# Landmark attention and a gated FFN on one core: landmark exchange in 256-byte pieces, Bm normalised from PSUM, R and a copy of Bm from one matmul, reciprocals kept in PSUM, and a new order of the stages

## The chip, the core and the metric

The kernel runs on one NeuronCore of a Trainium2 chip. Five engines work side by side, each through its own instructions in order: PE (TensorE, matmuls), DVE (VectorE), ACT (ScalarE), POOL (GpSimd) and SP (SyncE, which here only issues DMA transfers). They meet through semaphores. PE reads SBUF and writes PSUM; DVE and ACT read and write both; POOL reads and writes SBUF alone. The metric is device time in microseconds, the median of the runs shown; one more execution was profiled.

## What is computed

Eight batches of eight heads of attention with 32 landmarks, then a multiplicative FFN over all 4608 tokens:

```python
def _attn_ref(q, k, v):                       # (8, 8, 576, 64) each
    m = 32
    scale = 1.0 / np.sqrt(D)
    q_lm = q.reshape(B, H, m, S // m, D).mean(axis=3)
    k_lm = k.reshape(B, H, m, S // m, D).mean(axis=3)
    ...
    A = sm(q, k_lm)                           # softmax of scaled products
    Bm = sm(q_lm, k_lm)
    C = sm(q_lm, k)
    Z = Bm.transpose(0, 1, 3, 2) / (norm1(Bm) * norminf(Bm) + 1e-06)
    for _ in range(6):
        Z = 2 * Z - Z @ Bm @ Z
    return A @ Z @ C @ v

def _moe_ref(x, w1, w2, w3, w_out):           # x: 4608 x 512
    a = x @ w1
    b = x @ w2
    h = a * b @ w3
    return h @ w_out
```

## The kernel before

The program works batch by batch (number after the dot), and its order is written out by hand: ORDER is a list of 569 words, each of which emits the instructions of one stage on all the engines that the stage uses. Every engine then runs its instructions in the order in which the words emitted them, and there is no scheduler. The words, with the lines of the code before:

- LK, LQ (L105): load k or q of a batch as f16 through POOL's queue. LV (L124, L128): load v through SP's queue, four transfers. Two buffers each, so the load of batch b+2 waits until the readers of batch b are done.
- TK0, TK1, TQ0, TQ1 (L140): DVE transposes half of k or q in 32x32 blocks into qkT.
- SK, SQ (L189 to L195): POOL adds up the 18 tokens of each landmark, six instructions, into the tile lm (f16).
- E (L200): exchange. Each group of 32 partitions needs the landmark half that its neighbour group made. Four transfers from lm to lm on SP's queue move them, in pieces of 64 bytes (the 32 values of one head pair). They wait for POOL's last addition.
- B (L215 to L229): PE multiplies the landmarks of q and k into PSUM (small), ACT takes exp into SBUF (ebm), DVE sums (rbs), inverts, multiplies to bm and transposes to bt.
- C0, C1 (L242, L248, L250): landmarks of q against k, exp with a sum, transpose. A0, A1 (L289, L294): q against landmarks of k, exp.
- N (L256 to L265): column sums of bm by a matmul, their maximum inverted (nrn), and bm times nrn into the right half of sz. R (L274 to L280): bt times bt by 16 small matmuls; DVE scales the result into the left half of sz and adds 2I into tz.
- I0 to I5 (L363 to L373): the six steps of the iteration for Z, a chain PE, then DVE (tz) and ACT (sz), then PE.
- V0 to V2 (L310 to L322): exp(C) times v. D (L328): row sums of A into psD (small). Y0 to Y2 (L336): DVE inverts a third of them each, into rr in SBUF. X (L340, L342): DVE casts rr to f16 (rhi) and makes the mixed tile rmix. M0, M1 (L348, L351): PE spreads rmix, DVE multiplies A.
- Z (L380 to L386), G0 to G3 (L400 to L406): landmark values times w1 and w2. U0a to U7b (L413 to L419): both FFN factors by PE, ACT copies one out (a_sb), DVE multiplies (ab). W0.n, W1.n (L435, L444): the last product for 128 tokens, evicted by ACT and stored by two transfers on SP's queue.
- F: one piece of the fold of w3 with w_out into a single weight (L457 to L480), 64 pieces, which fill PE early on.

PSUM holds three tiles `big` of two banks, one `small` and one `acc`. So each new `small` (of B, N, R, D, Z) waits until the last one has been read.

The early words of ORDER, up to the second exchange (L32 to L35 of the code before; P and L3 load pieces of w3):

```
... TK0.0 F TK1.0 L3.3 F F F TQ0.0 P.4 L3.5 SK.0 ... TQ1.0 ...
... LV.0 ... TK0.1 F F SQ.0 F E.0 F TK1.1 SK.1 F F F F B.0 C0.0 C1.0 F F F N.0 A0.0 A1.0
TQ0.1 LK.2 LQ.2 R.0 ... I5.0 M0.0 LK.3 LQ.3 Z.0 M1.0 SQ.1 F G0.0 G1.0 E.1 ...
```

Of the kernel before, what the change touches and what calls it, by code (L numbers as in the profile page):

```python
# [31 lines left out]
F F F F F F F F F F F F F TK0.0 F TK1.0 L3.3 F F F TQ0.0 P.4 L3.5 SK.0 F F F F F TQ1.0 F F F F F  # L32
F F LV.0 F F F F TK0.1 F F SQ.0 F E.0 F TK1.1 SK.1 F F F F B.0 C0.0 C1.0 F F F N.0 A0.0 A1.0
TQ0.1 LK.2 LQ.2 R.0 L3.6 F F F V0.0 TQ1.1 I0.0 F I1.0 F F L3.7 I2.0 V1.0 D.0 Y0.0 Y1.0 Y2.0 F F
I3.0 F I4.0 V2.0 F F X.0 I5.0 M0.0 LK.3 LQ.3 Z.0 M1.0 SQ.1 F G0.0 G1.0 E.1 F F F TK0.2 TK1.2  # L35
SK.2 B.1 A0.1 C0.1 C1.1 F N.1 G2.0 G3.0 A1.1 F F TQ0.2 F F U0a.0 R.1 U0b.0 U1a.0 U1b.0 TQ1.2
LV.1 U2a.0 U2b.0 D.1 V0.1 U3a.0 I0.1 TK0.3 TK1.3 I1.1 U3b.0 V1.1 I2.1 U4a.0 Y0.1 SQ.2 Y1.1 Y2.1
E.2 I3.1 LK.4 LQ.4 X.1 U4b.0 I4.1 V2.1 M0.1 I5.1 U5a.0 TQ0.3 U5b.0 U6a.0 M1.1 Z.1 U6b.0 U7a.0
U7b.0 LV.2 G0.1 G1.1 B.2 G2.1 G3.1 W0.0 N.2 C0.2 C1.2 W1.0 SK.3 U0a.1 U0b.1 W0.1 TQ1.3 U1a.1
U1b.1 U2a.1 V0.2 R.2 A0.2 A1.2 SQ.3 LV.3 TK0.4 TK1.4 E.3 W1.1 I0.2 U2b.1 D.2 I1.2 Y0.2 Y1.2 Y2.2  # L40
V1.2 U3a.1 I2.2 W0.2 TQ0.4 U3b.1 U4a.1 TQ1.4 V2.2 I3.2 X.2 W1.2 U4b.1 I4.2 M0.2 W0.3 I5.2 B.3
SK.4 A0.3 U5a.1 U5b.1 Z.2 U6a.1 U6b.1 G0.2 G1.2 W1.3 M1.2 LK.5 LQ.5 U7a.1 U7b.1 G2.2 G3.2 W0.4
U0a.2 N.3 U0b.2 C0.3 C1.3 W1.4 A1.3 R.3 U1a.2 U1b.2 V0.3 I0.3 W0.5 U2a.2 TK0.5 U2b.2 V1.3 U3a.2
D.3 SQ.4 TQ0.5 Y0.3 E.4 I1.3 Y1.3 Y2.3 W1.5 U3b.2 U4a.2 TQ1.5 V2.3 LV.5 I2.3 W0.6 U4b.2 I3.3
U5a.2 W1.6 LV.4 LK.6 LQ.6 X.3 I4.3 U5b.2 U6a.2 I5.3 W0.7 Z.3 M0.3 M1.3 W1.7 U6b.2 TK1.5 SK.5
SQ.5 U7a.2 U7b.2 G0.3 G1.3 W0.8 LK.7 LQ.7 B.4 A0.4 G2.3 G3.3 U0a.3 W1.8 N.4 C0.4 C1.4 E.5 A1.4
R.4 W0.9 U0b.3 U1a.3 W1.9 U1b.3 I0.4 TK0.6 V0.4 V1.4 U2a.3 U2b.3 TK1.6 W0.10 U3a.3 I1.4 D.4 Y0.4
Y1.4 Y2.4 V2.4 U3b.3 U4a.3 W1.10 I2.4 U4b.3 U5a.3 U5b.3 I3.4 W0.11 X.4 U6a.3 I4.4 U6b.3 SK.6
LV.6 A0.5 I5.4 W1.11 M0.4 M1.4 Z.4 U7a.3 U7b.3 G0.4 G1.4 B.5 W0.12 G2.4 G3.4 U0a.4 W1.12 N.5
C0.5 A1.5 R.5 C1.5 W0.13 U0b.4 W1.13 I0.5 TQ0.6 V0.5 V1.5 W0.14 TQ1.6 SQ.6 U1a.4 E.6 TK0.7 TK1.7  # L50
U1b.4 W1.14 I1.5 V2.5 U2a.4 D.5 Y0.5 Y1.5 I2.5 U2b.4 U3a.4 TQ0.7 W0.15 I3.5 Y2.5 U3b.4 U4a.4 X.5
W1.15 SK.7 I4.5 U4b.4 U5a.4 M0.5 W0.16 TQ1.7 I5.5 U5b.4 U6a.4 M1.5 Z.5 U6b.4 SQ.7 U7a.4 U7b.4
G0.5 G1.5 W1.16 E.7 B.6 A0.6 G2.5 G3.5 W0.17 W1.17 N.6 C0.6 C1.6 A1.6 R.6 W0.18 U0a.5 U0b.5
U1a.5 U1b.5 W1.18 I0.6 D.6 Y0.6 Y1.6 Y2.6 V0.6 U2a.5 W0.19 U2b.5 U3a.5 W1.19 I1.6 U3b.5 V1.6
I2.6 W0.20 X.6 I3.6 M0.6 W1.20 I4.6 V2.6 U4a.5 I5.6 U4b.5 U5a.5 M1.6 Z.6 U5b.5 U6a.5 B.7 G0.6
# [10 lines left out]
def kernel(  # L66
# [83 lines left out]
    def constants():  # L150
# [29 lines left out]
        return mask4, eye, eye2, onesq, selc, lomask  # L180


    def landmarks(st, t):
        if "lm" not in st:
            st["lm"] = pat.tile([128, 2, 4, 2, 16, 2], FP16, name="lm", bufs=3)
# [8 lines left out]
        for xh in range(2):  # L194
            add(out=st["lm"][:, t, :, xh], in0=o[:, :, :, 0, :], in1=o[:, :, :, 1, :], op=ALU.add)  # L195

    def exchange(st):
        for to in range(4):
            p, r = slice(32 * to, 32 * to + 32), slice(32 * (to ^ 1), 32 * (to ^ 1) + 32)
            nc.sync.dma_start(  # L200
                out=st["lm"][p, :, :, 1 - to % 2].rearrange("p t c l e -> p (t c) (l e)"),
                in_=st["lm"][r, :, :, 1 - to % 2].rearrange("p t c l e -> p (t c) (l e)"))

    def lmk(st, sl, t, pr, e):
        return st["lm"][sl, t, pr].rearrange("p x l e -> p (x l) e")[:, :, e]

    def scores_b(st):
        psB = small()
        for qd in range(2):
            for e in range(2):  # L210
                for o in range(4):
# [7 lines left out]
        ebm = pz.tile([128, 2, 32], FP32, name="ebm")  # L219
        nc.scalar.activation(out=ebm, in_=psB[:, 0:64].rearrange("p (a m) -> p a m", m=32),  # L220
                             func=AXF.Exp, scale=SCALE / (GRP * GRP))
        rbs = pz.tile([128, 2], FP32, name="rbs")
        nc.vector.reduce_sum(out=rbs, in_=ebm, axis=AX.X)
# [4 lines left out]
        bt = st["bt"] = pz.tile([128, 2, 32], FP32, name="bt")  # L228
        nc.vector.transpose(out=bt, in_=bm)  # L229
# [23 lines left out]
    def norms(st):  # L253
# [10 lines left out]
        sz_ = st["sz"] = pz.tile([128, 2, 64], FP32, name="sz_")  # L264
        nc.vector.tensor_tensor(out=sz_[:, :, 32:64], in0=bm,  # L265
                                in1=nrn.unsqueeze(2).to_broadcast([128, 2, 32]), op=ALU.mult)

    def squares(st):
        psR = small()
        bt, sz_ = st["bt"], st["sz"]  # L270
        for qd in range(2):
            for h in range(4):
                sl = slice(32 * h, 32 * h + 32)
                nc.tensor.matmul(psR[sl, 32 * qd:32 * qd + 32], bt[sl, qd, :], bt[sl, qd, :],  # L274
                                 start=True, stop=True, tile_position=(32 * h, 32 * h))
        nc.vector.tensor_tensor(out=sz_[:, :, 0:32],
                                in0=psR[:, 0:64].rearrange("p (a m) -> p a m", m=32),
                                in1=st["nrn"].unsqueeze(2).to_broadcast([128, 2, 32]), op=ALU.mult)
        tz_ = st["tz"] = pz.tile([128, 2, 32], FP32, name="tz_")
        nc.vector.tensor_tensor(out=tz_, in0=sz_[:, :, 0:32], in1=eye2, op=ALU.add)  # L280
# [43 lines left out]
    def denominators(st):  # L324
# [7 lines left out]
        st["rr"] = pat.tile([128, QS], FP32, name="rr", bufs=1)  # L332

    def inverted(st, i):
        sl = slice(QS // 3 * i, QS // 3 * (i + 1))
        nc.vector.reciprocal(out=st["rr"][:, sl], in_=st["psD"][:, sl])  # L336

    def mixed(st):
        rhi = pat.tile([128, QS], FP16, name="rhi", bufs=1)
        nc.vector.tensor_copy(out=rhi, in_=st["rr"])  # L340
        st["rmix"] = pat.tile([128, QS], FP16, name="rmix")
        nc.vector.scalar_tensor_tensor(out=st["rmix"], in0=rhi, scalar=lomask[:, 0:1], in1=st["rr"],  # L342
# [155 lines left out]
    sts = [dict() for _ in range(B)]  # L498
# [52 lines left out]
    mask4, eye, eye2, onesq, selc, lomask = constants()  # L551
# [92 lines left out]
```

## Time and profile before

| | us |
|---|---|
| median of 3 runs | 283.25 (282.9 to 284.06) |
| the profiled execution | 283.65 |
| its span, first to last instruction | 281.9 |
| busy: PE | 261.5 (93%) |
| busy: DVE | 183.2 (65%) |
| busy: ACT | 132.2 (47%) |
| busy: POOL | 104.3 (37%) |

Busy time is the union of an engine's instructions; waiting on semaphores and issuing transfers are not in it. The page lists for each group of instructions the count, the busy time and the mean duration of one; the view of waits lists who waited for whom; the view by windows gives each engine's busy time in a stretch, with the granted TensorE clock (1.00 is full speed) and the busy share of the 16 DMA engines. That share can read above 1, since packets overlap. The view of one line or one tile gives shortest, median and longest duration, and for transfers the time from issue to landing.

### The profile page before, as it was taken

The numbers are of one execution on the slowest core, as the hardware profiler recorded it, in microseconds if no ns is written. First come the engines' busy times: TensorE is split into PE (matmuls) and PEld (weight loads), VectorE is DVE, ScalarE is ACT, GpSimd is POOL, SyncE is SP. The second block draws the span as 40 slices with busy tenths as digits, with TensorE's granted clock in tenths as the row PEclk, the third lists the DMA queues.
The fourth block names the chain that finished last, engine by engine and source line by source line (L and its number), as shares of the span: only waits on it lengthen the run. The fifth ranks groups of instructions, "written<-read, shape, count | busy, mean of one in ns | idle before, by whom it ended". The sixth has DMA issues, their size and how long they took to land.

```text
span 281.9 us, 10481 instructions
## 1 busy us (share of the span) xinstructions
PE 261.5 (93%) x4572; PEld 148.9 (53%) x4572; DVE 183.2 (65%) x397; ACT 132.2 (47%) x285; POOL 104.3 (37%) x125
## 2 busy tenths in 40 slices
PE   7999977999889499989999999999999999999992
PEld 3554533554456165546655655665565565645640
DVE  6764223558988477987769866889775685465510
ACT  3642222425543354556358444744673655436531
POOL 0719545451569119970009960089500000000000
PEclk9999997999999799999999999999999999999998
DMA  7999998886008925699494198114232723133144
GB/s 252 301 244 278 254 241 204 138 144 172 2 6 118 226 63 157 117 174 209 110 273 112 13 216 240 40 42 84 44 67 57 185 62 74 44 77 77 37 114 113
DMA packets 31246, 37.91 MB, mean 134 GB/s; under 512 B 10976, under 2 KB 19168, under 8 KB 31200
## 3 DMA queue, kind: packets, MB, share of 16 engines
q1 hardware_dynamic: 20864, 24.26, 33.3%
q0 software_dynamic: 9536, 11.54, 24.9%
q10 hardware_dynamic: 800, 1.44, 1.4%
q8 instruction: 36, 0.59, 0.9%
q14 instruction: 10, 0.08, 0.1%
HBM read 38.80 MB, written 9.44 MB: 171 GB/s over the span
## 4 chain that ended last, share of the span: by engine, by line
PE 61%; DMA 16%; POOL 9%; DVE 7%; SPq 2%; issue 1%; ACT 1%; ACTq 0%; POOLq 0%; DVEq 0%
PE acc L435 18%; PE big L413 17%; DMA lm<-lm 10%; PE big L400 6%; PE acc L477 5%; POOL tr L189 4%; PE big L310 3%; PE big L363 3%; DMA qkn<-in_k_dram 3%; DMA wof<-in_moe_w_out_dram 2%; DVE qkT L140 2%; POOL tr L190 2%; SPq L200 2%; PE big L242 2%; PE big L348 1%
## 5 line engine op out<-in xcount | busy, mean ns | idle before, releaser
L413 PE MATMUL big<-ahat,gt 128*128 128x288 f16 x512 | 74.7, 287 | 0.4 <-ACT a_sb L417 0.4
L435 PE MATMUL acc<-w,ab 128*128 128x512 f16 x264 | 67.8, 383 | 0.1
L419 DVE TENSOR_TENSOR ab<-a_sb,big 128x576 f16<-128x576 f16 x64 | 48.0, 750 | 23.0 <-ACT a_sb L417 12.3
L189 POOL TENSOR_TENSOR tr<-qkT 128x1024 f32<-128x1024 f16 x16 | 34.0, 2127 | 74.4 <-DVE qkT L140 74.1
L417 ACT CAST a_sb<-big 128x576 f16<-128x576 f32 x64 | 40.9, 640 | 39.3 <-PE big L413 38.7
L413 PEld LDWEIGHTS <-gt 128*128 128x128 f16 x512 | 47.2, 98 | 21.2 <-issue 3.1
L477 PE MATMUL acc<-wsp,w3t 128*128 128x512 f16 x168 | 41.3, 387 | 0.7 <-ACT w L480 0.7
L435 PEld LDWEIGHTS <-ab 128*128 128x128 f16 x288 | 25.7, 98 | 27.9 <-issue 5.8
L477 PEld LDWEIGHTS <-w3t 128*128 128x128 f16 x192 | 18.4, 99 | 21.7 <-issue 4.3
L444 ACT ACTIVATE o_sb<-acc 128x512 f32<-128x512 f32 x33 | 19.7, 598 | 15.0 <-PE acc L435 14.2
L140 DVE STREAM_TRANSPOSE qkT<-qkn 128x576 uint32<-128x576 uint32 x32 | 24.0, 763 | 1.6 <-DMA qkn<-in_k_dram 1.6
L406 DVE TENSOR_SCALAR gt<-big 128x1024 f16<-128x1024 f32 x16 | 19.4, 1218 | 5.2 <-PE big L400 4.9
L470 DVE SCALAR_TENSOR_TENSOR w3t<-big,w3t 128x512 f16<-128x512 f32 x16 | 11.0, 690 | 17.2 <-ACT w3t L469 17.0
L190 POOL TENSOR_TENSOR tr<-tr 128x512 f32<-128x512 f32 x16 | 20.3, 1269 | 1.3
L404 ACT ACTIVATE gt<-big 128x1024 f16<-128x1024 f32 x16 | 16.4, 1024 | 8.6 <-PE big L400 8.6
L400 PE MATMUL big<-wup,zt 64*32 64x512 f16 x512 | 17.8, 394 | 0.8 <-DVE ab L419 0.8
L310 PE MATMUL big<-vt,ent 64*32 64x64 f32 x1152 | 16.6, 224 | 0.0
L469 ACT ACTIVATE w3t<-big 128x512 f16<-128x512 f32 x16 | 9.5, 594 | 13.0 <-PE big L464 12.9
L310 PEld LDWEIGHTS big<-vt,ent 64*32 64x32 f32 x1152 | 13.2, 105 | 3.6 <-issue 1.6
L248 ACT ACTIVATE en<-big 128x288 f32<-128x288 f32 x32 | 12.7, 412 | 2.6 <-PE big L242 2.6
L250 DVE STREAM_TRANSPOSE ent<-en 128x576 f32<-128x576 f32 x16 | 12.2, 772 | 2.5 <-ACT en L248 2.5
L195 POOL TENSOR_TENSOR lm<-tr 128x128 f16<-128x128 f32 x32 | 12.1, 400 | 1.3
(277 smaller groups left out, 291.1 us busy)
## 6 DMA issues: line engine op xcount, KB each, us to landing
vt<-in_v_dram SPq DMA_DIRECT2D x32, 288.0 KB, 5.1
out_dram<-o_sb SPq DMA_DIRECT2D x71, 128.0 KB, 2.4
qkn<-in_k_dram POOLq DMA_DIRECT2D x8, 576.0 KB, 6.5
qkn<-in_q_dram POOLq DMA_DIRECT2D x8, 576.0 KB, 8.6
w3f<-in_moe_w_dram SPq DMA_DIRECT2D x6, 512.0 KB, 7.2
wup<-in_moe_w_dram POOLq DMA_DIRECT2D x4, 512.0 KB, 26.8
wof<-in_moe_w_out_dram ACTq DMA_DIRECT2D x4, 256.0 KB, 5.7
wof<-in_moe_w_out_dram SPq DMA_DIRECT2D x4, 256.0 KB, 4.1
```

Of the source, the lines that this page charges most:

```text
L140: nc.vector.transpose(out=st["qkT"][:, t, prs].rearrange("p c r q e -> p (c r q e)").bitcast(U32), in_=st["qkn"][:, t, prs, :].rearrange(" ...
L189: add(out=tr, in0=x[:, :, 0:4, :], in1=x[:, :, 4:8, :], op=ALU.add)
L190: add(out=tr[:, :, 0:2, :], in0=tr[:, :, 0:2, :], in1=tr[:, :, 2:4, :], op=ALU.add)
L310: nc.tensor.matmul(psV[32 * o:32 * o + 32, qd, 0:64], ent[sl, pr, r, :], vt[sl, pr, 64 * r:64 * r + 64], start=(r == 0), stop=(r == RT - 1 ...
L400: nc.tensor.matmul(psG[32 * h:32 * h + 32, qd, :], zt[rs, i, h, :], wup[rs, h, w, fs], start=(i == 0), stop=(i == 1), tile_position=(64 * ...
L406: nc.vector.tensor_scalar(out=g[:, :, w, fs], in0=psG, scalar1=1.0 / ZS, scalar2=None, op0=ALU.mult)
L413: nc.tensor.matmul(p[:, c, 0:HS], st["g"][:, qd, w, 128 * j:128 * j + 128], st["ahat", qd][:, c, :], start=(qd == 0), stop=(qd == 1))
L417: nc.scalar.copy(out=st["a_sb"], in_=p[:, :, 0:HS])
L419: nc.vector.tensor_tensor(out=st["ab"][:, j, st["t0"]:st["t0"] + S].rearrange("p (c s) -> p c s", c=2), in0=st["a_sb"], in1=p[:, :, 0:HS], ...
L435: nc.tensor.matmul(pso[:, :], ab[:, j, t0:t0 + 128], w34[:, j, :], start=(j == 0), stop=(j == 7))
L444: nc.scalar.activation(out=o_sb[:, c], in_=pso[:, c], func=AXF.Copy, scale=1.0 / (X64 * X64))
L477: nc.tensor.matmul(psW[j][:, :], turned[j, c // 4][:, a, c % 4, :], wsp[:, b, c, :], start=(c == 0 and a + b == 0), stop=(c == 7 and a == 1))
```

## The change

Five things are changed.

1. The tile lm is laid out anew, [tensor][half][landmark][head pair][parity] in place of [tensor][head pair][half][landmark][parity]. The half that a partition group sends is then 256 contiguous bytes for each of q and k. The exchange is still four transfers of 16 KB in all 64 KB, each from 32 partitions, with 64 pieces in place of 256. POOL's last additions write, and the matmuls of A, B and C read, the tile with a step of 8 elements (16 bytes) where it was 2 (4 bytes).
2. B: the exponentials go into PSUM, beside the scores in the same bank, by two ACT instructions with an accumulated sum in place of one without. The DVE sum goes. bm is made from PSUM. bt is the left half of one of two constant tiles whose right half is the identity.
3. N and R: the DVE product bm times nrn in N goes. The 16 matmuls of R are 64 columns wide, and give R and bm side by side. tz comes from two DVE instructions (multiply by nrn, add 2I), sz from one of 128 elements.
4. Y and X: the reciprocals are written beside the row sums in PSUM; the cast to f16 goes from DVE to ACT, and rmix reads PSUM.
5. ORDER has the same 569 words in another order.

```diff
-... TK0.0 F TK1.0 L3.3 F F F TQ0.0 P.4 L3.5 SK.0 ... TQ1.0 ...
-... LV.0 ... TK0.1 F F SQ.0 F E.0 F TK1.1 SK.1 F F F F B.0 C0.0 C1.0 F F F N.0 A0.0 A1.0
-TQ0.1 LK.2 LQ.2 R.0 L3.6 F F F V0.0 TQ1.1 ... LK.3 LQ.3 Z.0 M1.0 SQ.1 F G0.0 G1.0 E.1 F F F TK0.2 TK1.2
-SK.2 B.1 A0.1 C0.1 C1.1 F N.1 G2.0 G3.0 A1.1 F F TQ0.2 F F U0a.0 R.1 U0b.0 ... TQ1.2
-LV.1 ... U4a.0 Y0.1 SQ.2 Y1.1 Y2.1
-E.2 I3.1 LK.4 LQ.4 ...
...
-W1.15 SK.7 ... SQ.7 U7a.4 U7b.4
-G0.5 G1.5 W1.16 E.7 B.6 ...
+F F F F F F F F L3.3 F F F F F TK0.0 TK1.0 F F F F F F F TQ0.0 F P.4 TQ1.0 F F F F L3.5 F F SK.0
+F TK0.1 F F F F LV.0 F F F F F F F F F TK1.1 SQ.0 E.0 B.0 C0.0 C1.0 F F L3.6 N.0 TQ0.1 F A0.0
+A1.0 R.0 F F F TQ1.1 I0.0 V0.0 F I1.0 F F I2.0 F D.0 SK.1 Y0.0 Y1.0 V1.0 LK.2 I3.0 LQ.2 Y2.0 F
+L3.7 F X.0 SQ.1 E.1 F I4.0 V2.0 F LV.1 TK0.2 I5.0 M0.0 F Z.0 M1.0 F G0.0 TK1.2 LK.3 G1.0 LQ.3
+TQ0.2 F SK.2 F F TQ1.2 B.1 C0.1 C1.1 A0.1 F G2.0 G3.0 SQ.2 E.2 A1.1 F F N.1 F U0a.0 ...
...
+M0.5 ... G0.5 G1.5 TK1.7
+W1.16 G2.5 G3.5 B.6 A0.6 W0.17 W1.17 N.6 C0.6 C1.6 SK.7 A1.6 R.6 W0.18 U0a.5 U0b.5 TQ1.7 SQ.7
+U1a.5 E.7 W1.18 ... U5b.5 U6a.5 U6b.5 B.7
...
+        bte = [consts.tile([128, 2, 64], FP32, name=f"bte{i}") for i in range(2)]
+        for t in bte:
+            nc.vector.tensor_copy(out=t[:, :, 32:64], in_=eye)
...
-            st["lm"] = pat.tile([128, 2, 4, 2, 16, 2], FP16, name="lm", bufs=3)
+            st["lm"] = pat.tile([128, 2, 2, 16, 4, 2], FP16, name="lm", bufs=3)
...
-            add(out=st["lm"][:, t, :, xh], in0=o[:, :, :, 0, :], in1=o[:, :, :, 1, :], op=ALU.add)
+            add(out=st["lm"][:, t, xh].rearrange("p l c e -> p c l e"), in0=o[:, :, :, 0, :],
+                in1=o[:, :, :, 1, :], op=ALU.add)
 
     def exchange(st):
-        for to in range(4):
-            p, r = slice(32 * to, 32 * to + 32), slice(32 * (to ^ 1), 32 * (to ^ 1) + 32)
-            nc.sync.dma_start(
-                out=st["lm"][p, :, :, 1 - to % 2].rearrange("p t c l e -> p (t c) (l e)"),
-                in_=st["lm"][r, :, :, 1 - to % 2].rearrange("p t c l e -> p (t c) (l e)"))
+        halves = st["lm"].rearrange("(a h i) t x l c e -> h a i t x (l c e)", a=2, h=2)
+        for ph in range(2):
+            for a in range(2):
+                nc.sync.dma_start(out=halves[ph, a, :, :, 1 - ph, :], in_=halves[1 - ph, a, :, :, 1 - ph, :])
 
     def lmk(st, sl, t, pr, e):
-        return st["lm"][sl, t, pr].rearrange("p x l e -> p (x l) e")[:, :, e]
+        return st["lm"][sl, t, :, :, pr, e].rearrange("p x l -> p (x l)")
...
-        ebm = pz.tile([128, 2, 32], FP32, name="ebm")
-        nc.scalar.activation(out=ebm, in_=psB[:, 0:64].rearrange("p (a m) -> p a m", m=32),
-                             func=AXF.Exp, scale=SCALE / (GRP * GRP))
         rbs = pz.tile([128, 2], FP32, name="rbs")
-        nc.vector.reduce_sum(out=rbs, in_=ebm, axis=AX.X)
+        ebm = psB[:, 64:128].rearrange("p (a m) -> p a m", m=32)
+        for qd in range(2):
+            nc.scalar.activation(out=ebm[:, qd, :], in_=psB[:, 32 * qd:32 * qd + 32], func=AXF.Exp,
+                                 scale=SCALE / (GRP * GRP), accum_out=rbs[:, qd:qd + 1])
...
-        bt = st["bt"] = pz.tile([128, 2, 32], FP32, name="bt")
-        nc.vector.transpose(out=bt, in_=bm)
+        bt = st["bt"] = bte[st["b"] % 2]
+        nc.vector.transpose(out=bt[:, :, 0:32], in_=bm)
...
-        sz_ = st["sz"] = pz.tile([128, 2, 64], FP32, name="sz_")
-        nc.vector.tensor_tensor(out=sz_[:, :, 32:64], in0=bm,
-                                in1=nrn.unsqueeze(2).to_broadcast([128, 2, 32]), op=ALU.mult)
...
-                nc.tensor.matmul(psR[sl, 32 * qd:32 * qd + 32], bt[sl, qd, :], bt[sl, qd, :],
+                nc.tensor.matmul(psR[sl, 64 * qd:64 * qd + 64], bt[sl, qd, 0:32], bt[sl, qd, :],
                                  start=True, stop=True, tile_position=(32 * h, 32 * h))
-        nc.vector.tensor_tensor(out=sz_[:, :, 0:32],
-                                in0=psR[:, 0:64].rearrange("p (a m) -> p a m", m=32),
-                                in1=st["nrn"].unsqueeze(2).to_broadcast([128, 2, 32]), op=ALU.mult)
         tz_ = st["tz"] = pz.tile([128, 2, 32], FP32, name="tz_")
-        nc.vector.tensor_tensor(out=tz_, in0=sz_[:, :, 0:32], in1=eye2, op=ALU.add)
+        for qd in range(2):
+            nc.vector.scalar_tensor_tensor(
+                out=tz_[:, qd, :], in0=psR[:, 64 * qd:64 * qd + 32], scalar=nrn[:, qd:qd + 1],
+                in1=eye2[:, qd, :], op0=ALU.mult, op1=ALU.add)
+        sz_ = st["sz"] = pz.tile([128, 2, 64], FP32, name="sz_")
+        nc.vector.tensor_tensor(out=sz_, in0=psR[:, 0:128].rearrange("p (a m) -> p a m", m=64),
+                                in1=nrn.unsqueeze(2).to_broadcast([128, 2, 64]), op=ALU.mult)
...
-        st["rr"] = pat.tile([128, QS], FP32, name="rr", bufs=1)
 
     def inverted(st, i):
         sl = slice(QS // 3 * i, QS // 3 * (i + 1))
-        nc.vector.reciprocal(out=st["rr"][:, sl], in_=st["psD"][:, sl])
+        nc.vector.reciprocal(out=st["psD"][:, QS + sl.start:QS + sl.stop], in_=st["psD"][:, sl])
 
     def mixed(st):
         rhi = pat.tile([128, QS], FP16, name="rhi", bufs=1)
-        nc.vector.tensor_copy(out=rhi, in_=st["rr"])
+        rr = st["psD"][:, QS:2 * QS]
+        nc.scalar.copy(out=rhi, in_=rr)
         st["rmix"] = pat.tile([128, QS], FP16, name="rmix")
-        nc.vector.scalar_tensor_tensor(out=st["rmix"], in0=rhi, scalar=lomask[:, 0:1], in1=st["rr"],
+        nc.vector.scalar_tensor_tensor(out=st["rmix"], in0=rhi, scalar=lomask[:, 0:1], in1=rr,
                                        op0=ALU.mult, op1=ALU.add)
```

## The prediction

> **What bounds the kernel now.** I read the slices first, then the waits of PE, then the stretches around them, then the rows of the tiles that are changed.
>
> ```profile
> PE   7999977999889499989999999999999999999992
> PEclk9999997999999799999999999999999999999998
> PE small L215 <- DMA lm<-lm: 7.1, 4, 3.3
> PE small L256 <- DVE bm L226: 1.4, 1, 1.4
> PE big L289 <- DMA lm<-lm: 1.0, 1, 1.0
> PE big L400 <- DVE ab L419: 0.8, 1, 0.8
> ...
> 40.00:50.00 10.00, 6.63 (x113) 3.35 (x112) 3.69 (x12) 2.35 (x10) 5.93 (x8) 0.83 0.97 209
> 90.00:100.00 10.00, 6.24 (x117) 2.86 (x123) 4.94 (x9) 2.91 (x4) 2.49 (x5) 0.83 0.97 196
> ```
>
> The first two lines are 40 slices of busy PE and of its granted clock. PE is full nearly everywhere, 93% over the span. The holes of the middle are few, and the waits name them (total, times, longest): 8.1 us for the landmark exchange, lm to lm, in batches 0, 2 and 5; 1.4 us once for bm; and six smaller waits for DVE or ACT of 0.2 to 0.8 us, 3.1 in sum. In the two 10 us stretches (after the length: busy PE, weight load, DVE, ACT, POOL, then the clock) the large exchange waits are followed by a mean clock of 0.83, which is 10 x 0.17 = 1.7 us of full-speed time lost each. The stretches of 10 us without such a wait show 1.00. So an exchange wait costs its length and, twice, 1.7 us more: 8.1 + 3.4 = 11.5 us. PE's own work is what remains and can't shrink by waiting less.
>
> ```profile
> L200 SPq DMA_DIRECT2D lm<-lm x4: 609/628/706, 85.4 to 87.4; - x4
> DMA to landing us min/median/max: 4.6/7.9/8.5
> ...
> L200 SPq DMA_DIRECT2D lm<-lm x4: 608/628/666, 189.7 to 191.8; - x4
> DMA to landing us min/median/max: 1.9/1.9/2.0
> ...
> DMA packets 31246, 37.91 MB, mean 134 GB/s; under 512 B 10976, under 2 KB 19168, under 8 KB 31200
> ```
>
> These are two exchanges out of eight (ns of an issue, shortest, median, longest; then us to landing). With little else in flight a transfer lands 1.9 us after its issue; beside two 576 KB loads of qkn it takes 8.5. Four issues of about 0.65 us follow one another on SP, so a quiet exchange takes 189.7 to 193.7, 4 us, and a loaded one 10.5. Eight exchanges of 64 KB in 64-byte pieces are 8192 of the 10976 packets below 512 bytes.
>
> **Exchange.** The issues stay four, so the 4 us of a quiet one stay: 3 x 0.65 + 1.9. Only the excess under load, 6.5 us, can go with the pieces. If it is one turn among the other queue's packets per piece, a quarter of the pieces leaves 6.5 / 4 = 1.6, and an exchange under load takes 5.6 us. If it is only waiting behind older bytes, it keeps 10.5. I take the first, because the load is the only difference between the two rows above. For batch 0 the wait also contains v: SP has issued four 288 KB transfers of v at 26.6 to 28.8, which lie ahead on the same queue.
>
> Batch by batch, with the new order. *Batch 0:* in the old order TK1.0 on DVE waits behind one w3t, so that POOL begins SK.0 at 20.58; the two transposes now follow one another (17.71 and 18.50), so SK.0 begins near 19.3. SQ.0 is then held by TQ1.0, which stays behind the same w3t and ends at 25.85, and starts there in place of 26.52. Six additions take 5.9 us (2.12 + 1.27 + 0.72 + 0.67 + 0.76 and gaps), so E.0 is issued at 31.8 in place of 32.4. v lies 1.3 us earlier on SP's queue, as its release follows SK.0. The old exchange ended 44.5, 5.3 us after v had landed at 39.2; of that I keep 1.9 and a quarter of 3.4, 2.75, on 38: 40.8. PE has 41 fold pieces before B.0 in both orders and arrives at 40.8. The 3.3 us stall becomes 0 to 1; I charge 0.5, and no slow clock.
> *Batch 2:* SQ.2 and E.2 move from behind Y2.1 to in front of A1.1. From the next batch's stages in the PE rows (a fold piece 0.7, turned pieces 1.2, V 0.66, G 1.0, I 0.27) TK1.2 comes at about 62, SK.2 runs to 69, SQ.2 to 75, and the exchange lands by 81 even under load (5.6), against PE's arrival at B.2 near 87. Stall gone.
> *Batch 5:* LK.6 and LQ.6 are issued before SK.5, no longer beside the exchange at 159.7, and TK1.5 comes some eight stages earlier. Its 1.0 us goes.
> What the moves push back: SK.1 behind TK1.1 ends 47.2 (was 44.8), so the loads LK.2, LQ.2 queued behind it on POOL start 2.5 us late and land near 53 and 56, just before TK0.2 and TQ0.2 need them (57, 62). LK.3, LQ.3 go behind SQ.1: issued near 55 instead of 52.9, needed after 75. LV.2 and LV.3 on SP follow E.2, no longer in front. SK.7, SQ.7, E.7 move late: from TK1.7 to landing I count 9.7 (until TQ1.7) + 5.9 + 4 = 19.6 us, while PE has nine halves of W (0.87), 14 halves of U (0.54) and 9 us of small stages, 24.4 in all, before B.7. Cover 4.8 us; if that exchange were slow (10.5) the stall would be 1.7. Sum of this part: -8.1 - 3.4 + 0.5 = -11.0.
>
> **B, N, X.** These rows (shortest, median, longest ns) show why bm was waited for:
>
> ```profile
> L226 DVE TENSOR_TENSOR bm<-ebm,rbs x8: 224/225/1950, 45.6 to 223.6; 128x64 f32<-128x64 f32 x8
> L342 DVE SCALAR_TENSOR_TENSOR rmix<-rhi,lomask,rr x8: 367/370/1384, 62.2 to 247.8; 128x144 f16<-128x144 f16 x8
> L340 DVE CAST rhi<-rr x8: 224/232/681, 61.9 to 247.5; 128x144 f16<-128x144 f32 x8
> ...
> L321 DVE TENSOR_TENSOR xs<-big,rcr x8: 291/292/292, 61.7 to 246.5; 128x128 f32<-128x128 f32 x8
> ```
>
> Operations on SBUF alone stretch up to nearly nine times; the 1.95 us one starts at 69.39, with POOL's 2.1 us addition running from 69.14. The one that reads PSUM (L321) never leaves 292. Busy time over count x median is 4.4 us for bm, 1.4 for rmix, 1.0 for rhi, and 1.4 for the sz and tz products of N and R: 8.2 us of DVE that the PSUM operands should free. On PE this is worth the 1.4 us at L256, whose N.1 also moves behind G2.0, G3.0 and A1.1 (2.4 us of PE). The rest is slack on DVE: over 60 to 100 us it is about 78% busy, and between 70 and 90 about 90%, so it is cover against new waits, priced at nothing.
> The other side: ACT in B runs two pieces with accumulator (a pair of L248's kind comes every 0.39 us) for one of 0.22, +0.56 us, DVE's sum of 0.22 goes; B to bm is 0.3 us longer, hidden by C. X crosses from DVE to ACT and back, about 0.3 us more than 0.23 + 0.37; M0 lies 1.4 us of PE or more behind X everywhere (least after X.4: two halves of U and I3.4). ACT then stands at rhi until Y2 is through, and behind it the a_sb copies, for whose DVE product PE waits via `big`. I charge 1.5 us for such new waits, between 0 and 6.4 (0.8, the largest of that kind now, in each of eight batches). psD is now held from D to X; B, N, R and Z of no batch fall between, so it costs nothing.
>
> **R.** 16 matmuls of 32 columns become 64 wide. The I stages are such: 0.27 us of PE from start to next start, against 0.24 for R. +0.03 x 8 = 0.3. DVE: tz by two 32-wide pieces (0.18 each, as the 64-wide PSUM product of L276 at its shortest) and sz of 128 (0.29), for 0.18 + 0.23 and N's 0.23: even.
>
> **lm with step 8.**
>
> ```profile
> L242 PEld LDWEIGHTS <-lm x256: 87/89/140, 44.6 to 233.7; 32*32 32x32 f16 x128
> L400 PEld LDWEIGHTS <-zt x512: 88/89/148, 65.3 to 255.2; 64*32 64x32 f16 x171
> ```
>
> Step 2 (lm) and step 1 (zt) load equally fast, so a step of 4 bytes is free. No row has 16 bytes. The weight loads of lm are 3.4 + 3.4 + 1.7 = 8.5 us busy. Below: 0, as the rows of both steps agree. Above: each further 89 ns on a load adds 8.5 if nothing hides it. They run pulled ahead under other tiles' matmuls; I take 0.5, nearer the measured steps. POOL writes with the new step too; 0.40 us each, 32 of them, off the path.
> [...]
>
> **Smaller waits.** Of the 3.1 us I let half go, since the order around each is new and others will come: -1.5.
>
> **Sum.** 281.9 - 11.0 - 1.4 + 1.5 + 0.3 + 0.5 - 1.5 = 270.3 of span. The profiled execution took 283.65, 1.75 beyond its span, and lies 0.4 above the median: 270.3 + 1.75 - 0.4 = 271.6.
>
> **Rivals.**
> *The pieces don't matter* (12%): the exchange waits behind older bytes. For it: in batch 0 the first landing (41.8) comes after v's last. Against: batch 2 has none of v ahead and is as slow. Batches 2 and 5 are rescued by the order, batch 0 keeps 3.3 + 1.7 less the 0.5 charged: 276.1.
> *DVE or ACT becomes the bound* (14%): the PE waits gone squeeze 90% of DVE at 70 to 90 us into less time, and ACT's wait in X holds copies. Against: 8.2 us less DVE work. With the full 6.4 us of new waits and the 1.5 not recovered: 271.6 + 4.9 + 1.5 = 278.
> *lm reads slow PE* (10%), the one on the other side: if a load's time grew with its step, four times as far would be four times as long, with nothing to hide it: 3 x 8.5 = 25.5 us, 271.6 + 25 = 296.6. It decides from (283.25 - 271.6 + 0.5 + 1.4) / 8.5 = 1.6, loads 2.6 times as long (229 ns). For it: no row excludes it; against: steps 1 and 2 are equal.
> *The forecast*: 60%, 266 to 274. The remaining 4% are slower by something unseen in the late order, B.7 first.
>
> **Range and chances.** Low end: all of 3.1 gone, no new waits, lm free: 271.6 - 1.6 - 1.5 - 0.5 - 0.5 = 267.5, and 1.5 for an estimate of PE rows that hide small gaps: 266. High end 280, which takes in the first two rivals and loads of lm twice as long (271.6 + 8.5 - 0.5 = 279.6). 0.5% (1.4 us) is what this measurement tells from no change. Faster: 60 + 12 + 8 of the second's 14 + 1 = 81%; same 6%, slower 13% (10 + 3).
>
> **What would show it.** Right: exchanges of four issues landing within 6 us, no PE wait on lm above 1 us, clock 1.00 from 10 to 270 us; L226's successor near 225 ns at most; DVE below 178 us busy; PE idle below 6 us in the middle. Wrong: weight loads from lm above 150 ns; waits of PE on ACT or DVE above 5 us in sum; a stall at B.7; batch 0 landing after 43.

## The result, and the profile after

| | before | after |
|---|---|---|
| median, us | 283.61 (281.19 to 285.24, 18 runs) | 281.23 (278.0 to 286.8, 18 runs) |
| ratio | | 0.9883, 95% interval [0.9849, 0.9917] |
| profiled execution, us | 283.65 | 282.19 |
| its span, us | 281.9 | 280.2 |
| span less busy PE, us | 281.9 - 261.5 = 20.4 | 280.2 - 262.7 = 17.5 |
| busy DVE, ACT, us | 183.2, 132.2 | 174.5, 136.1 |

The changed kernel is 1.2% faster by this ratio, which leaves out the slow runs, those more than 1.5% above a kernel's fastest (7 of the 18 of the changed kernel), and 0.8% faster by the medians of all runs (281.23 against 283.61). Either is more than the 0.5% which the prediction took as what can be told from no change, but the median is 10 us above the forecast of 271.6, and 1.2 us above the top of the range. The first view is the page's 40 slices of busy PE and of its granted clock; lines of the changed kernel are numbered 3 higher from B on (E is L205). The profiled execution lies 1 us above its median.

```profile
PE   7999989899978998997999999899999999999992
PEclk9999999999997999998999999999999999999997
```

The deep holes after 40 us are gone, shallower ones are spread over the whole middle, and the clock still drops twice. The waits of PE in the changed kernel (in all, times, longest):

```profile
PE big L366 <- issue: 3.7, 3, 1.9
PE big L416 <- issue: 1.7, 1, 1.7
...
PE big L292 <- issue: 1.1, 1, 1.1
...
PE big L351 <- PE big L366: 0.7, 1, 0.7
...
PE small L218 <- DMA lm<-lm: 0.6, 1, 0.6
```

The wait for lm fell from 8.1 to 0.6 us, and the one for bm is gone. In their place stand five waits of 6.5 us in sum which end with no event that the profile shows ("issue"); for the kernel before the same view lists none. Two stretches of 10 us of the changed kernel, in which such a wait stands (length, busy PE, weight load, DVE, ACT, POOL, clock, DMA share, GB/s):

```profile
80.00:90.00 10.00, 7.72 (x151) 5.21 (x152) 6.34 (x16) 3.31 (x8) 3.47 (x6) 0.83 1.13 246
130.00:140.00 10.00, 9.21 (x161) 5.27 (x161) 5.04 (x13) 3.63 (x9) 7.23 (x7) 0.83 0.41 76
```

The mean clock of 0.83, which in the kernel before was the mark of a long wait for lm, is here again: 1.7 us lost each, as before, in other places. Then the exchanges of batches 0 and 2, and the rows of the tiles lm and bm in the changed kernel:

```profile
L205 SPq DMA_DIRECT2D lm<-lm x4: 594/604/709, 31.9 to 34.0; - x4
DMA to landing us min/median/max: 7.2/7.3/7.6
L205 SPq DMA_DIRECT2D lm<-lm x4: 595/658/950, 76.3 to 78.6; - x4
DMA to landing us min/median/max: 3.5/6.1/6.9
```

```profile
L245 PEld LDWEIGHTS <-lm x256: 129/131/158, 41.6 to 231.7; 32*32 32x32 f16 x128
L218 PE MATMUL small<-lm x128: 218/229/252, 40.8 to 220.7; 32*32 32x32 f16 x128
...
L229 DVE TENSOR_TENSOR bm<-small,rbs x8: 225/225/226, 43.0 to 221.9; 128x64 f32<-128x64 f32 x8
```

The exchange of batch 0 lands at 41.55 (forecast 40.8). That of batch 2 under load takes 8.7 us from first issue to last landing, not 5.6, but is issued at 76.3 in place of 85.4, so that PE doesn't wait for it. bm is at 225 ns in all eight batches, where the longest was 1950. The weight loads from lm in C and A went from 89 and 88 to 131 ns, those in B from 88 to 151 (medians; 151 is above the 150 ns that the prediction gave as a sign of being wrong), and B's matmuls from 173 to 229.

### The profile page after: what moved, and what is told of

It reads as the page before. It is cut to its first block, busy times and chain, and to the rows that moved or that the text cites. A ratio compares the mean times of both kernels' runs of the same rounds, so it can differ in the third digit from the quotient of the medians.

```text
span 280.2 us, 10514 instructions
## 1 busy us (share of the span) xinstructions
PE 262.7 (94%) x4572; PEld 150.6 (54%) x4572; DVE 174.5 (62%) x383; ACT 136.1 (49%) x317; POOL 104.4 (37%) x125
## 4 chain that ended last, share of the span: by engine, by line
PE 83%; DMA 5%; issue 3%; ACT 2%; DVE 2%; POOL 2%; SPq 1%; ACTq 0%; POOLq 0%
PE big L416 24%; PE acc L438 21%; PE acc L480 8%; PE big L403 6%; PE big L313 5%; PE big L366 5%; DMA lm<-lm 3%; PE big L292 2%; PE small L480 2%; PE big L351 2%; PE big L245 2%; PE big L467 2%; DMA w3f<-in_moe_w_dram 1%; PE big L438 1%; PE small L383 1%
## 5 line engine op out<-in xcount | busy, mean ns | idle before, releaser
L416 PE MATMUL big<-ahat,gt 128*128 128x288 f16 x512 | 76.0, 290 | 2.1 <-issue 1.7
L403 PE MATMUL big<-wup,zt 64*32 64x512 f16 x512 | 17.1, 379 | 0.2 <-ACT en L251 0.2
L472 ACT ACTIVATE w3t<-big 128x512 f16<-128x512 f32 x16 | 9.5, 594 | 14.5 <-PE big L467 14.4
L354 DVE TENSOR_TENSOR ahat<-eat,big 128x576 f16<-128x576 f16 x16 | 11.9, 752 | 3.6 <-PE big L351 3.4
```

The lines of the kernel that those rows point to most:

```text
L403: nc.tensor.matmul(psG[32 * h:32 * h + 32, qd, :], zt[rs, i, h, :], wup[rs, h, w, fs], start=(i == 0), stop=(i == 1), tile_position=(64 * ...
L416: nc.tensor.matmul(p[:, c, 0:HS], st["g"][:, qd, w, 128 * j:128 * j + 128], st["ahat", qd][:, c, :], start=(qd == 0), stop=(qd == 1))
```

## What the "issue" waits are

The timeline of PE around the longest of them, in the changed kernel (start, length, engine and line, what it writes and reads, count, and in brackets the wait before):

```profile
128.31 0.31 PE L331 MATMUL small<-eat,onesq 128*32 128x144 f16 x8
128.55 0.30 PE L366 MATMUL big<-sz__2368,tz__2366 32*32 32x64 f32 x5
130.79 0.45 PE L366 MATMUL big<-sz__2368,tz__2366 32*32 32x64 f32 x11 [1.95 <-issue]
```

PE stops after 5 of the 16 matmuls of one I step. All 16 read the same two tiles, sz and tz, each made by one instruction, and write one tile. So it is hardly data that PE waits for. The page has a DMA queue q8 of kind "instruction", and the DMA view of two stretches before PE goes on shows when it moved something (packets, MB, share of 16 engines):

```profile
q8 instruction: 36, 0.59, 0.9%
```

```profile
q0 software_dynamic: 558, 0.63, 76.6%
q1 hardware_dynamic: 215, 0.41, 30.8%
```

```profile
q0 software_dynamic: 134, 0.15, 72.1%
q1 hardware_dynamic: 90, 0.14, 37.6%
q8 instruction: 1, 0.02, 5.0%
```

The first line is the whole span: 36 packets of 16 KB. PE has 4572 matmuls and as many weight loads; 0.59 MB over 9144 is about 64 bytes, so that a packet would be some 256 of PE's instructions. The next two lines are 123.2 to 128.6 us: no such packet came, while packets of q0, the queue of the q and k loads, took 77% of the 16 engines' time. The last three lines are 128.5 to 129.7. Here one came; by the trace it ended at 129.59, and PE went on at 130.79. Each of the five waits ends 1.2 to 1.4 us after such a packet. Theory T is therefore: PE's instructions arrive in packets of 256 on the DMA engines that carry the loads; where a packet is late and PE has just done many short matmuls, it runs out of instructions. The rival is a wait that belongs to its place in the program and that the records don't show.

## The experiments

Each was timed beside the kernel before on its chip (medians there 283.3 to 284.0 us), in 6 to 12 runs.

**Without the q, k and v loads from batch 2 on**, for the kernel after and the one before:

```diff
-        "LK": lambda st, b: load_qk(st, b, 1), "LQ": lambda st, b: load_qk(st, b, 0),
-        "LV": lambda st, b: first_v() if b == 0 else load_v(st, b),
+        "LK": lambda st, b: load_qk(st, b, 1) if b < 2 else st.update(qkn=sts[b % 2]["qkn"]),
+        "LQ": lambda st, b: load_qk(st, b, 0) if b < 2 else None,
+        "LV": lambda st, b: ... load_v(st, b) if b < 2 else st.update(vt=sts[b % 2]["vt"]),
```

> The changed kernel without the loads of q, k and v from batch 2 on: those batches compute with the tiles of batches 0 and 1, everything else is as it was. Theory (PE runs out of its own instructions when their fetch by DMA is held up by the loads): the PE waits put down to 'issue' (6.5 us in the changed kernel's profile, five of them) fall below 0.5 us in sum after 60 us, the clock shows 1.00 throughout the middle, and the time is 281.2 - 6.5 - 3.4 = 271, between 268 and 274. Rival (the waits come from PE's instructions themselves, such as weight loads with a step of 16 bytes or a hazard between small matmuls): the 'issue' waits stay at 5 us or more and the time is 278 or more.

> The kernel before without the loads of q, k and v from batch 2 on (tiles of batches 0 and 1 in their place). Theory (loads hold up the exchange, whatever its pieces): the exchanges of batches 2 and 5 land within 4.5 us of their first issue in 64-byte pieces too, PE's waits for lm fall from 8.1 to 3.5 us (batch 0 stays), one of the two stretches of slow clock goes: 283.6 - 4.6 - 1.7 = 277, between 274 and 279. Rival (64-byte pieces are slow by themselves): exchanges of 8 us or more stay, time within 1 us of 283.6.

After: 270.56 us (ratio 0.9542, [0.9494, 0.9591]), before: 275.62 (0.9716, [0.9671, 0.976]). The changed kernel without these loads has no "issue" wait left and no slow clock before its end:

```profile
80.00:90.00 10.00, 9.89 (x237) 5.84 (x237) 8.64 (x18) 5.91 (x17) 2.10 (x4) 1.00 0.01 3
```

So the waits come from the loads. That 270.56 is near the forecast of 271.6 doesn't confirm it: without these loads the kernel before gains 8 us too, as expected (its waits for lm fall from 8.1 to 3.3), and the change is worth 5.1 us, not 11.7.

**The order alone, the edits alone.** ORDER of the one kernel in the other, with nothing else:

> The changed kernel with the old ORDER. If the 256-byte pieces make a loaded exchange short (my forecast's step): exchanges of batches 0, 2 and 5 land within 6 us of their first issue, PE waits for lm 2 us at most, no slow clock, time 274 to 277. If an exchange waits behind older bytes whatever its pieces (the rival): landings stay at 8 to 12 us there, PE waits for lm stay above 5 us with two stretches of slow clock, and the wider R and the slower weight loads of lm add 1 to 3 us: time 282 to 286.

> The kernel before with the new ORDER alone: 64-byte pieces, old B, N, R, Y and X. If the order is what takes the exchange off PE's path: PE waits for lm below 3 us, 'issue' waits of PE of 4 us or more as in the changed kernel, and a time of 277 to 282, no worse than the changed kernel. If the pieces are needed for it: PE waits for lm above 5 us, time 283 or more.

The edits in the old order: 279.74 us (0.9855, [0.9802, 0.9908]), "issue" waits 1.6, waits for lm 2.5, and still two slow stretches; the time lies between the two expectations. The new order without the edits: 284.5 us (0.9998, [0.9961, 1.0035]), where 277 to 282 was expected. There the waits for lm fall to 3.0 (2.4 of it in batch 0), and "issue" rises to 7.1:

```profile
PE small L215 <- DMA lm<-lm: 3.0, 3, 2.4
PE big L413 <- issue: 2.1, 1, 2.1
PE big L363 <- issue: 2.0, 2, 1.8
PE big L289 <- issue: 1.5, 1, 1.5
```

The new order exchanges one kind of wait for another, and wins nothing as long as the loads run. Of the kernels here with all loads uncut and the warm-up as it was, those in the new order have 6.5 to 7.1 us of "issue" (with the parted loads of the attempt below 6.8), those in the old order 0 to 1.8.

**Is it the place or the packet?** In this kernel only the warm-up at the start is cut up, so that all later packet boundaries shift by half a packet:

```diff
         for _ in range(n):
-            nc.tensor.matmul(psw[:, 0, :], warm[:, 0:128], warm, start=True, stop=True)
+            for i in range(6):
+                s = slice(88 * i, min(88 * i + 88, 512))
+                nc.tensor.matmul(psw[:, 0, s], warm[:, 0:128], warm[:, s], start=True, stop=True)
```

> The changed kernel with each of its 12 warm-up matmuls on zeros cut into six of 88 columns: 60 more matmuls, so about 120 more instructions on PE, all in the first 10 us, and nothing else touched. Theory T (PE's own instructions arrive as packets of 16 KB, 256 instructions each, on the DMA engines, and PE runs dry when one is late): the boundaries of the packets move by half a packet against the program, so the five waits of the changed kernel put down to 'issue' (3.7 us at L366, 1.7 at L416, 1.1 at L292) do not come back at their places: at least three of the five end at another step or are gone, and new ones may stand elsewhere; their sum is anywhere from 1 to 9 us and the time from 276 to 285. Rival (these waits belong to their places in the code, a semaphore or a read that the records do not show): the same five waits before the same steps, each within 0.4 us of its size, and 281 us.

278.73 us (0.9821, [0.9769, 0.9873]). None of the five waits is at its place. Three others, 2.8 us in sum, stand at V and G steps. The timeline of PE where the longest of the five had been (the I step is whole again, V is broken):

```profile
129.93 0.69 PE L313 MATMUL big<-vt,ent 64*32 64x64 f32 x45
131.27 0.24 PE L313 MATMUL big<-vt,ent 64*32 64x64 f32 x2 [0.64 <-issue]
...
131.53 0.34 PE L366 MATMUL big<-sz__2502,tz__2500 32*32 32x64 f32 x16
```

That the five have moved is not the scatter of runs: the changed kernel, profiled again on another chip, has all five before the same matmuls (0.75, 1.79, 1.07, 1.94 and 1.39 us; 0.82, 1.73, 0.90, 1.95 and 1.11 in the first profile) and one more of 0.18.

The traces also allow a count. Three windows of the changed kernel and two of this one go from the start of the span into such a wait; the first two counts in each line are PE's matmuls and weight loads up to there:

```profile
0.00:84.50 84.50, 77.04 (x1112) 41.57 (x1113) 51.33 (x133) 34.59 (x82) 50.03 (x65) 1.00 0.89 202
0.00:110.00 110.00, 101.33 (x1623) 55.85 (x1623) 70.68 (x173) 47.12 (x114) 62.63 (x79) 0.98 0.85 191
0.00:130.00 130.00, 119.85 (x2005) 67.02 (x2006) 85.35 (x201) 58.87 (x142) 69.66 (x87) 0.99 0.82 185
```

```profile
0.00:82.80 82.80, 76.23 (x1112) 43.52 (x1113) 50.07 (x129) 33.95 (x81) 49.37 (x64) 1.00 0.88 202
0.00:131.10 131.10, 122.10 (x2133) 70.98 (x2134) 87.11 (x205) 60.46 (x145) 71.46 (x88) 1.00 0.83 186
```

Their sums are 2225, 3246 and 4011 when the 8th, 12th and 15th packet of q8 comes, and here 2225 and 4267 at the 8th and 16th: 255 to 255.3 a packet. With the other instructions that the trace has of PE (39 in all, nearly all on semaphores) it is 256. The other two waits of the changed kernel, which end at 54.96 and 176.50, stand at 950 and 5798, when the 3rd and the 22nd packet comes: 255 and 255.3 a packet again. At the count of 2225 the program with the cut warm-up is 120 instructions earlier in its steps, and PE stops there too. The waits follow the count of instructions, and the rival is out.

**Which edit.** The exchange and the layout of lm alone, all other edits without them (both in the old order), and the exchange alone in the new order. Their diffs are parts of the change as shown above.

> The kernel before with the new layout of lm and the exchange in pieces of 256 bytes, and nothing else. Theory T: waits for lm fall from 8.1 to 2 to 4 us, the lm weight loads rise to about 130 ns, the wait for bm of 1.4 us stays: 280 to 282 us. Rival 'pieces do not matter': waits for lm of 7 us or more, and 284 to 285.5 us with the slower weight loads.

> The edits to B, N, R, Y and X with the old order of steps and the old exchange: lm in the old layout, pieces of 64 bytes. To stand beside the 279.74 us of all edits in the old order. Theory T (the pieces win back most of the waits for lm, and the layout costs 1.5 to 2 us in slower weight loads): lm weight loads at 87 ns and B's matmuls at 171 again, waits for lm of 6 to 8 us in place of 2.5, no wait for bm: 282 to 283.5 us. Rival 'pieces do not matter': waits for lm under 4 us and 277 to 279 us. Rival 'the pieces are all there is': 283.6 us, as before.

> The kernel before with the exchange in pieces of 256 bytes (278.4 us with the old order of steps) and the new order, without the other edits. Theory (the new order starts q's and k's loads where PE's steps are many and short, so it adds 'issue' waits): 4 us or more of 'issue' waits and 280 to 283 us. Rival (the other edits are what the changed kernel loses against 278.4 us): 276 to 279 us.

| us (ratio to before) | old order | new order |
|---|---|---|
| no edit | 283.3 to 284.0 | 284.5 (0.9998) |
| pieces of 256 bytes alone | 278.4 (0.9801), again 279.63 (0.9865) | 280.9 (0.9882) |
| all other edits | 284.42 (1.0007) | not run |
| all edits | 279.74 (0.9855) | 281.23 (0.9883), again 281.48 (0.9921) |

With the pieces alone in the new order "issue" is 6.7 us, and the time is as expected. The pieces alone do at least as much as the whole change; the other edits by themselves, with 64-byte pieces and in the old order, give nothing that can be measured (1.0007, [0.9971, 1.0043]); in both rows of the table that have the pieces the new order reads 1.3 to 2.5 us longer, with intervals that touch. The waits of PE with the pieces alone, then with all but the pieces:

```profile
PE small L215 <- DMA lm<-lm: 2.3, 3, 1.1
PE big L348 <- issue: 1.8, 1, 1.8
PE big L400 <- DVE ab L419: 1.4, 1, 1.4
```

```profile
PE small L218 <- DMA lm<-lm: 6.8, 4, 2.7
PE big L366 <- issue: 1.8, 2, 1.3
```

With the pieces, waits for lm fall to 2.8 (with 0.5 at L289) and this execution has no slow clock left in the middle. Without them they are 7.8 (with 1.0 at L292). The three loaded exchanges of the old order, from first issue to last landing, took 12.1, 10.5 and 10.1 us before (batches 0, 2 and 5), and take 10.0, 8.2 and 9.2 with the pieces alone.

**Parts of the rest, without loads.** R undone (its lines of the change's diff taken back), and the old order, both without the loads from batch 2 on and with the other edits:

> The changed kernel without the loads from batch 2 on (270.56 us) and with R undone: its matmuls give 32 columns again, bm is scaled by nrn in N. Theory (R's 64 columns of FP32 cost the 0.14 us a batch by which 16 of its matmuls grew from 0.26 to 0.40 us): 1.1 us less, 269.2 to 269.8 us. Rival (R's cost is small or made good by the DVE work it saves): 270.2 to 271 us.

> The changed kernel without the loads from batch 2 on, with the old order of steps. Theory (without loads in the way the new order has nothing to avoid but 1 to 1.5 us of small waits of M, W and N): 271 to 272.5 us. Rival (the new order is worth 3 us or more by itself where the loads don't disturb it): 273.5 us or more. Rival (it is worth nothing at all): 270 to 270.9 us.

R undone: 270.37 against 270.56 us, so R costs nothing that shows. The old order: 275.09 us (0.9674, [0.9633, 0.9714]). My 271 to 272.5 was too low: where no loads are in the way the new order is worth 4.5 us, about 2.7 of waits and 1.7 of one slow stretch after batch 0's exchange. With the loads all of it is lost again (281.23 us in the new order, 279.74 in the old).

**Which loads.** First an attempt to part them, so that fewer are in flight at once, which missed: LQ.2, LQ.3, LQ.5, LQ.6 and LQ.7 moved behind the next landmark sum on POOL, TQ.6 later, and LV.2 to LV.6 moved in between. For batches 2 and 3:

```diff
-... SK.1 Y0.0 Y1.0 V1.0 LK.2 I3.0 LQ.2 ... SQ.1 E.1 ... LK.3 G1.0 LQ.3 TQ0.2 F SK.2 ... SQ.2 E.2 ... LV.2 ... LV.3
+... SK.1 Y0.0 Y1.0 V1.0 LK.2 I3.0 ... SQ.1 LQ.2 E.1 ... LK.3 G1.0 TQ0.2 F SK.2 LQ.3 ... LV.2 SQ.2 E.2 ... W1.0 LV.3
```

> The changed kernel with q's and k's loads parted (q's load stands behind another landmark sum on POOL, some 6 us after k's) and the v loads of batches 2 to 6 set between them; the same work, the same bytes. [...] Rival (what delays the packets is the mean traffic, which is unchanged): 'issue' waits of 5 us or more and 280 to 284 us.

280.53 us (0.9873, [0.9823, 0.9924]), "issue" 6.8 us: no better, and what the rival, the mean traffic, had expected. Then either kind left out (only the LV line, or only the LK and LQ lines, of the diff of the first experiment):

> The changed kernel without the v loads of batches 2 to 7 (the tiles of batches 0 and 1 serve again); q's and k's loads stay. It tells which transfers delay PE's instruction packets. Theory Tv (the v loads on SP's queue, four of 288 KB a batch, are what they wait behind): 'issue' waits fall from 6.5 us to under 2, no slow clock before 260 us, 271 to 274 us. Rival Tqk (q's and k's loads of 576 KB on POOL's queue): 'issue' waits stay at 4 us or more, 277 to 281 us. If both count in part: 274 to 277 us.

> The counterpart: without the q and k loads of batches 2 to 7, the v loads stay. Theory Tv: 'issue' waits of 4 us or more and 277 to 281 us. Rival Tqk: under 2 us of them, 271 to 274 us. Loaded exchanges: 8.5 us as in the changed kernel by Tv, under 6 us by Tqk.

Without v 277.71 us (0.9753, [0.9703, 0.9804]) with 3.8 us of "issue"; without q and k 272.23 (0.9588, [0.9554, 0.9622]) with 1.0. Either leaves out 7.1 of 37.9 MB as the DMA packets count them. The same stretch without v, then without q and k:

```profile
80.00:90.00 10.00, 7.78 (x201) 5.36 (x208) 7.57 (x18) 4.25 (x14) 3.58 (x6) 1.00 0.58 97
```

```profile
80.00:90.00 10.00, 9.89 (x250) 5.97 (x251) 8.65 (x18) 5.59 (x15) 2.33 (x5) 1.00 0.79 201
```

With v alone the packets of this stretch move twice as many bytes and keep the engines busier (0.79 against 0.58), and PE is full. So a busy share as such doesn't hold PE up; it is mostly the q and k loads that do: q0's transfers of 576 KB, cast to f16, in pieces of 1152 bytes. But they are counted as f16 and lie in HBM as f32. The pages' lines of what was read from HBM fall from 38.8 MB to 31.7 without v and to 24.6 without q and k. So the q and k loads read twice as much, and that this is what delays a packet is not excluded.

**Shorter, parted loads.** Each q and k load of batches 2 to 7 in two halves, with POOL's additions or a dummy one between them, many of them at other places in ORDER than before; then the same with more distance in batches 6 and 7 and the v loads moved as in the attempt above; and this again with the cut warm-up. The diff has batch 6 with the greater distance.

```diff
+    def spacer():
+        nc.gpsimd.tensor_tensor(out=idle, in0=idle, in1=idle, op=ALU.add)
...
-LQ.2 ... SQ.1 E.1 ... LK.6 ... LQ.6
+SQ.1 PQ0.2 SP PQ1.2 E.1 ... SQ.4 PK0.6 SP SP PK1.6 SP SP PQ0.6 SP SP PQ1.6
```

PK0 and PK1 load the halves of k, PQ0 and PQ1 those of q, SP is the dummy.

> The changed kernel with each q and k load of batches 2 to 7 cut into two of 288 KB, and about 2 to 3 us of POOL time set between any two of them: an adding step of the landmark sums where there is one, a dummy addition on an idle tile (128x704 FP32, estimated at 1.7 us from the 1.27 us of 128x512 and the 2.13 us of 128x1024) where there is none. The same bytes in all. Theory (an instruction packet waits behind what the q and k loads have in flight, so shorter and parted loads make it wait less): 'issue' waits under 2.5 us, 273 to 276.5 us, against 281.2 us of the changed kernel and 272.2 us without q's and k's loads. Rival (it waits as long as there is any such load, and parting them only makes that time longer): 'issue' waits of 5 us or more and 279 to 283 us. Rival (the halves come too late for the transposes, and DVE holds up the rest): new PE waits on DVE over 2 us.

> The kernel with halved and parted q and k loads (277.5 us), with twice the dummy work between the halves of batches 6 and 7 (4 to 5 us apart, about what one half takes to land) and the v loads of batches 2 to 6 moved out of the k and q loads' way. Theory (it is what is in flight at one time that an instruction packet waits behind): 'issue' waits fall from 4.1 us to under 2 us, 273 to 276 us. Rival (parting helps only while the load in question is short; the mean traffic does the rest): 'issue' waits stay at 3 us or more and 276.5 to 279 us.

> The same with the 12 warm-up matmuls cut into six pieces each, which moves the packet boundaries by half a packet. Theory T: what 'issue' waits are left stand at other steps, and the time is within 2.5 us of the same without it, in either direction. Rival (the cut warm-up is itself a gain, as 278.7 against 281.2 us might be read): at least 1.5 us less than without it.

> The changed kernel once more, unedited, on the chip of these other kernels, so that they stand beside it directly: 279.5 to 282.5 us, 0.985 to 0.992 of the kernel before. If it is under 279 us, the differences of 2 to 4 us to the parted loads and to the pieces alone are no more than chips and runs make.

> The kernel before with the exchange in pieces of 256 bytes and nothing else, once more beside the changed kernel: 277 to 279.5 us, and 2 to 4 us under the changed kernel if the pieces alone are worth more than all the edits with the new order. Rival (the 278.4 us were a lucky lie of the packets on that chip): within 1 us of the changed kernel.

The halves: 277.52 us (0.9761, [0.9723, 0.9799]), "issue" 4.1 us, between the first two expectations. With more distance: 275.13 us (0.9724, [0.9672, 0.9776]), beside 281.48 (0.9921, [0.9878, 0.9963]) for the changed kernel and 279.63 (0.9865, [0.98, 0.9931]) for the pieces alone on one chip. This version is the fastest of those that load everything, 2.3% below the changed kernel. With the cut warm-up 276.13, one such wait left, of 1.2 us at another place, and a slow stretch after batch 0's exchange: half a packet more or less decides little here. The waits of PE in the fastest:

```profile
PE big L335 <- issue: 1.9, 1, 1.9
...
PE big L438 <- DVE wbd L398: 1.1, 1, 1.1
PE big L388 <- issue: 0.9, 2, 0.6
```

2.8 us of "issue" are left, not the under 2 that I expected, and the slow stretches in the middle are gone. The changed kernel's profiled execution on this chip (283.14 us) had 7.1 us of "issue" and both stretches: 4.3 + 3.4 = 7.7 of the 7.9 us by which this one (275.2) is shorter; by the medians 6.4 us are won. The same bytes are loaded, which speaks against the mean traffic. What did it, the halves, their distance, or the new places of the loads, was not parted. That the pieces alone beat the whole change is not settled: 1.9 us apart on this chip, with intervals that overlap.

## Why the prediction was too low

- **The step that failed** is "What the moves push back". There I followed the moved loads on POOL and SP to the transposes that need them, and not to what else uses the DMA engines. The rivals were a bound by DVE, slow reads and useless pieces; none was a wait for instructions. So the waits of PE for its own instructions stand in the sum at nothing. Span less busy PE was to fall by 9.0 us (-8.1 + 0.5 - 1.4 + 1.5 - 1.5), and fell by 2.9; the 6.5 us of "issue" are that gap of 6.1.
- **The slow clock, -3.4:** not won. The two stretches come back with waits for instructions. Busy PE was to fall by 2.6 (-3.4 + 0.3 + 0.5) and rose by 1.2.
- **The waits for lm, -8.1 + 0.5:** right in sum (0.6 left), for a reason half wrong. A quarter of the pieces doesn't leave a quarter of the excess: loaded, the exchange of batch 2 went from 10.5 to 8.7 us, not 5.6, and in the old order the pieces alone take 0.9 to 2.3 us off a loaded exchange, where 4.9 was forecast. The rest of the cover is the earlier issue, and it is in that order that the loads delay the packets of instructions.
- **bm, -1.4:** the wait is gone, as forecast, and DVE freed by 8.7 us (forecast 8.2). But with all edits except the pieces the time is that of before, so the 1.4 us don't show in it; the rest, which I priced at nothing, was worth nothing that shows.
- **New waits for DVE and ACT, +1.5:** hardly any came. The one larger new wait, 0.7 at L351, is put down to PE's own I step; a wait of 0.7 for sz was there before. ACT didn't become a bound.
- **R, +0.3:** its undoing, without the loads, shows no difference (0.2 us, on another chip).
- **lm with step 8, +0.5:** too small. Busy time of B's matmuls went from 2.9 to 3.8 us, of A's and C's from 14.4 to 15.4: up to 1.9 us. The loads in A and C took 1.47 times as long (131 against 89 ns), those in B 1.7 times (151 against 88). No run shows loads of lm twice as long, which the upper end of the range took in (8.5 - 0.5 us more): by the medians 1.7 times is the most.
- **B.7** showed no stall, as forecast: the one wait for lm left is batch 0's.
- **The rivals:** "the pieces don't matter" is refuted (279.74 with them, 284.42 without, same order); loads of 229 ns did not come (the longest took 158).

## What to carry to other kernels

Before a stall is moved, list everything that shares the resource behind it; on the DMA engines here that includes PE's own instructions, at one packet per 256 of them. A wait in the middle of a group of matmuls with the same operands may be a wait for instructions: whole packets of instructions between two such waits show it from the trace alone, and adding 120 instructions early tells it in one run. Cutting large loads and setting them apart won 6.4 us here, and an order that gains 4.5 us without the loads gained nothing with them.

## What the runs showed that I had not expected

- PE waits much for its instructions beside q0's loads (3.8 us with q and k alone) and little beside those of v on q1 (1.0), which write as many bytes (7.1 MB either) and read half as many (7.1 MB against 14.2). Which property of the q and k loads counts (twice as many pieces, 1152 bytes each against 2304, the cast and the bytes read for it, the queue of another kind, software_dynamic) was not tried.
- The clock drops to half (0.50) with some waits of PE (1.73 and 1.95 us in the changed kernel) and not with others as long (1.8 with the pieces alone, where the mean clock of the whole execution is 0.997, and 1.9 in the fastest version, where it is 1.000). Each of the four drops between 40 and 260 us, two in the kernel before (from 44.56 and 95.76) and two in the changed one (from 85.95 and 130.32), lasts 3.41 us. From the end of the first to the second it is 47.8 us before and 41.0 after, 14 and 12 times 3.41. The 3.41 us ahead of the first drop of the changed kernel, and as long a stretch of the fastest version, each with a long wait in it:

```profile
82.54:85.95 3.41, 1.68 (x34) 1.22 (x28) 1.21 (x6) 1.09 (x3) 1.16 (x3) 1.00 1.17 274
147.05:150.46 3.41, 1.73 (x112) 1.17 (x111) 2.05 (x4) 0.86 (x2) 3.31 (x4) 1.00 1.12 235
```

  PE is busy for 0.49 of the first and for 0.51 of the second, which no drop follows. In the 3.41 us ahead of the other drops it was busy for 0.57 (changed kernel, from 126.91) and for 0.11 and 0.06 (kernel before, from 41.14 and 92.34); 0.60 in the kernel before (68.45 to 71.87) was followed by none. So 0.57 had a drop behind it and 0.51 none, and what decides it stays open.
- With little else in flight small pieces cost next to nothing: over all exchanges the shortest landing is 1.9 us with pieces of 64 bytes and 1.8 with 256. The longest fell from 10.9 to 7.6 us, but the median rose from 3.3 to 5.7: in the new order five exchanges take over 8 us, where three took over 10.
